# Coarse attention of two heads in three pieces of 96 keys instead of four of 72

## The chip, the cores and the metric

The program runs on one core of a Trainium2 chip. The metric is device time in microseconds (us) of one execution. The engines are TensorE (PE in the rows; PEld is its weight load), VectorE (DVE), ScalarE (ACT), GpSimd (POOL) and SyncE (SP, whose queue issues nearly all DMAs here). They run side by side and wait for one another by semaphores.

## The reference

An attention block feeds two feed-forward layers. q, k and v have 4 batches, 8 heads, 576 tokens and 64 channels, all in float32.

```python
q_d = q.reshape(B, H, Sd, 4, D).mean(axis=3)      # likewise k_d and v_d: Sd = 144 coarse tokens
out_d = softmax(q_d @ k_d.T / sqrt(D)) @ v_d
out_up = np.repeat(out_d, 4, axis=2)
mask = np.abs(pos[:, None] - pos[None, :]) < 4     # local part: a band of seven keys
out_local = softmax(where(mask, q @ k.T / sqrt(D), -1e9)) @ v
x = (out_up + out_local)                           # to (2304, 512)
h = x @ w_in;  x = (h * sigmoid(h)) @ w_out                # first layer, 512 -> 2048 -> 512
h = x @ w2_in; out = (h * sigmoid(1.702 * h)) @ w2_out     # second layer
```

The weights of both layers are given as float64 and are converted on the chip.

## The kernel before, in words

The two layers are float16 products in two parts each (a high and a low half; three products stand for one). They are the lines L709, L840 and L868 (first layer) and L902 and L981 (second layer). The attention is computed in float32. It is cut into 32 units: a unit is one pair of heads (of four, `NHP`) in one half of a batch's queries (eight halves, `NM`), so a unit has 288 queries, of which come 72 coarse queries (`PD` = 72), against 144 coarse keys per head.

A unit runs through these steps, each a small function. `scores` (L1247 coarse, L1254 local) fills a PSUM tile with both kinds of scores. `dmax`, `dexp` and `dnorm` make the coarse probabilities `pd`, a tile of 72 queries by two heads by 144 keys. `dtr` (L1313) transposes it on TensorE in four pieces of 72 keys, two for each head, into one PSUM bank; `dcp` (L1317) copies these to SBUF as `pdT`. `av` (L1330) multiplies each piece by the pooled values `vd` (72 keys by 64 channels): head 0 writes partitions 0 to 63 of the result, head 1 partitions 64 to 127, and the two pieces of a head add up in PSUM. Behind it `av` issues the 24 local products (L1336) on tiles of 32 rows and 64 columns. TensorE carries out each float32 product as two passes, so four coarse products are eight matmuls in the trace; a transpose is one.

The pooled values of a pair of heads are made once per batch. For batch 0 `vsum` (L1198) sums the value windows `vw`, which the local part has loaded anyway, by matmuls with a constant of zeros and ones, `T["vsum"]`, made by a GpSimd memset (L1046) and VectorE reductions (L1052) at the start; `vcp` (L1202) copies the result out of PSUM. For the batches 1 to 3 `lv` (L1091) loads v with four tokens in a row into the tile `vraw`, of which there is one buffer, and `sv` (L1180, L1181) adds the four tokens on GpSimd. The next `lv` waits until `sv` has read the tile.

The order of all steps on all engines is fixed by a string of places (`PLACES`) that lists the steps; the costs noted with each step do not change that order. Each engine works through its own instructions in that order. On SyncE the loads `lv` stand between the loads of k (L1076), q (L1076), value windows (L1125), weights (L523, L604) and the stores of converted weights (L632).

Of the kernel before, what the change touches and what calls it, by code (L numbers as in the profile page):

```python
# [8 lines left out]
F32 = mybir.dt.float32  # L9
# [14 lines left out]
BAND = 4  # L24
# [75 lines left out]
class Plan:  # L100
# [7 lines left out]
    def add(self, name, eng, dur, fn, r=(), w=(), alloc=(), lock=False, mb=0.0, after=(), nd=1):  # L108
        s = Step()
        s.name, s.eng, s.dur, s.fn, s.lock, s.mb = name, eng, dur, fn, lock, mb  # L110
        s.deps, s.succ, s.alloc, s.n, s.nd = {}, [], list(alloc), len(self.steps), nd
        for a in after:
            s.deps[a] = False
        for k in r:
            for p in self.last.get(k, ()):
                s.deps[p] = True
            self.readers.setdefault(k, []).append(s)
        for k in w:
            for p in self.last.get(k, ()):
                s.deps[p] = True  # L120
            for p in self.readers.get(k, ()):
                if p is not s:
                    s.deps[p] = True
            self.last[k] = [s]
            self.readers[k] = []
        for tag, key, *_ in alloc:
            self.tags[key] = tag
        s.keys = set(r) | set(w)
        for k in s.keys:
            self.users.setdefault(k, []).append(s)  # L130
        self.steps.append(s)
        return s
# [87 lines left out]
def kernel(ctx: ExitStack, tc: tile.TileContext, q, k, v, w1_in, w1_out, w2_in, w2_out, out):  # L220

    nc = tc.nc
    B, H, S, D = q.shape
    NT, DM = out.shape
    DFF = w1_in.shape[1] // 2
    P = 128
    NHP = H // 2
# [4 lines left out]
    T2 = 256  # L232
    D2 = DM // 2
    PD = HALF // BAND
    QB = 24
    TT = 96
    NBL = HALF // TT
# [9 lines left out]
    add = plan.add  # L247
# [8 lines left out]
    pools = {}  # L256
    T = {}
# [6 lines left out]
    DVE, ACT, POOL = nc.vector, nc.scalar, nc.gpsimd  # L264
# [758 lines left out]
    def attention_init():  # L1023
        ac = pools["ac"]
        T["ident"] = const.tile([P, P], F32, name="ident")
        make_identity(nc, T["ident"])
        T["cap"] = ac.tile([P, 2 * NBL, 32], F32, name="cap")
        T["big"] = x2[:, 0, 0:P].rearrange("p (i k) -> p i k", i=4)
        POOL.memset(T["big"], 3.0e38)
        for sign in (1, -1):  # L1030
            POOL.affine_select(out=T["big"], in_=T["big"], pattern=[[32 * sign, 4], [sign, 32]], compare_op=ALU.is_ge,
                               fill=8.0 * NEG, base=BAND - 1 - sign * BAND, channel_multiplier=-sign)
        T["kTs"] = [ac.tile([P, S + 2 * BAND], F32, name=f"kT{i}") for i in range(NHP)]
        for t in T["kTs"]:
            POOL.memset(t[:, 0:BAND], 0.0)
            POOL.memset(t[:, BAND + S:], 0.0)
        T["qTs"] = [ac.tile([P, HALF + PD], F32, name=f"qT{i}") for i in range(2)]
        for t in T["qTs"]:
            POOL.memset(t[:, HALF:], 0.0)
        T["smr"] = [ac.tile([P, 8, 2], F32, name=f"smr{i}") for i in range(2)]  # L1040
        T["smi"] = [ac.tile([P, 8], F32, name=f"smi{i}") for i in range(2)]
        for t in T["smr"]:
            POOL.memset(t[:, :, 0], 1.0)
            POOL.memset(t[:, :, 1], 1e-9)
        T["vsum"] = ac.tile([P, 3, PD], F32, name="vsum")
        POOL.memset(T["vsum"], 0.0)  # L1046
        T["four"] = ac.tile([P, TT + 2 * QB], F32, name="four")

    def init_cap():
        cap = T["cap"]  # L1050
        for e in range(3):
            DVE.tensor_reduce(out=T["vsum"][:, e, QB * e:QB * (e + 1)].rearrange("p (i t) -> p i t", i=4),  # L1052
                              in_=T["ident"].rearrange("p (i j) -> p i j", i=4)[:, :, BAND:BAND + QB].rearrange("p i (t r) -> p i t r", r=BAND),
                              axis=AX.X, op=ALU.add)
        DVE.tensor_copy(out=T["four"][:, QB:QB + TT], in_=T["ident"][:, :TT])
        DVE.tensor_reduce(out=T["four"][:, :QB], in_=T["ident"][:, :TT].rearrange("p (t r) -> p t r", r=BAND), axis=AX.X, op=ALU.add)
        DVE.tensor_scalar(out=T["four"][:, QB + TT:], in0=T["four"][:, :QB], scalar1=SCD, scalar2=None, op0=ALU.mult)
        for i in range(4):
            r = slice(32 * i, 32 * i + 32)
            DVE.tensor_copy(out=cap[r], in_=T["big"][r, i, :].unsqueeze(1).to_broadcast([32, 2 * NBL, 32]))  # L1060
        DVE.memset(cap[0:32, 0, 0:BAND], 8.0 * NEG)
        DVE.memset(cap[96:128, 2 * NBL - 1, 32 - BAND:], 8.0 * NEG)
# [16 lines left out]
                nc.sync.dma_start(out=t[:TT].rearrange("p (c h d) -> p c h d", h=2, d=D)[:, :, hh], in_=src[hh].rearrange("(c p) d -> p c d", p=TT))  # L1079

    def load_kv(b, hp):
        h = slice(2 * hp, 2 * hp + 2)
        nm = f"{b}.{hp}"

        def lk():
            T["kraw" + nm] = pools["ld"].tile([P, S + 2 * TT], F32, tag="kraw", name="kraw")
            load_tokens(T["kraw" + nm], [k[b, 2 * hp + hh] for hh in range(2)], S, blocked(2 * b))

        def lv():
            T["vraw" + nm] = pools["ld"].tile([PD, 4, BAND * D], F32, tag="vraw", name="vraw", bufs=1)  # L1090
            nc.sync.dma_start(out=T["vraw" + nm], in_=v[b, h].rearrange("h (c p r) d -> p (h c) (r d)", p=PD, r=BAND))  # L1091

        n0 = len(plan.steps)
        add("lk" + nm, "SP", 0.44, lk, w=["kraw" + nm], alloc=[("kraw", "kraw" + nm)], mb=1.0 if blocked(2 * b) else 0.69, nd=4 if blocked(2 * b) else 2)
        if b:
            add("lv" + nm, "SP", 0.36, lv, w=["vraw" + nm], alloc=[("vraw", "vraw" + nm)], mb=0.33)
        if b:
            for s in plan.steps[n0:]:
                plan.soft.append((w1_loaded, s))
# [51 lines left out]
    def keys_of(b, hp):  # L1151
        nm = f"{b}.{hp}"
        kps, kT, kd, vd = "kps" + nm, "kT" + nm, "kd" + nm, "vd" + nm
# [21 lines left out]
                              in_=src.rearrange("p c (t r) -> p c t r", r=BAND), axis=AX.X, op=ALU.add)  # L1175

        def sv():
            T[vd] = pools["at"].tile([PD, 4, D], F32, tag="vd", name="vd", bufs=NHP)
            vr = T["vraw" + nm].rearrange("p j (r d) -> p j r d", r=BAND)
            POOL.tensor_tensor(out=vr[:, :, 0:2, :], in0=vr[:, :, 0:2, :], in1=vr[:, :, 2:4, :], op=ALU.add)  # L1180
            POOL.tensor_tensor(out=T[vd], in0=vr[:, :, 0, :], in1=vr[:, :, 1, :], op=ALU.add)  # L1181
# [8 lines left out]
        vps = "vps" + nm  # L1190

        def vsum():
            T[vps] = bank1("vps")
            o = T[vps][:PD, :4 * D].rearrange("p (h c d) -> p c h d", h=2, c=2)
            vw = T["vw" + nm].rearrange("p (h c e) d -> p c e h d", h=2, c=2)
            for c in range(2):
                for e in range(3):
                    nc.tensor.matmul(o[:, c], T["vsum"][:, e], vw[:, c, e], start=e == 0, stop=e == 2)  # L1198

        def vcp():  # L1200
            T[vd] = pools["at"].tile([PD, 4, D], F32, tag="vd", name="vd", bufs=NHP)
            ACT.copy(out=T[vd].rearrange("p j d -> p (j d)"), in_=T[vps][:PD, :4 * D])  # L1202

        if b:
            add("KV" + nm, "POOL", 2.1, sv, r=["vraw" + nm], w=[vd], alloc=[("vd", vd)])
# [4 lines left out]
    def unit(u):  # L1210
# [96 lines left out]

        def dtr():
            T[tps] = bank1("tps")
            for hh in range(2):  # L1310
                for kc in range(2):
                    j = 2 * hh + kc
                    nc.tensor.transpose(T[tps][:PD, j * PD:(j + 1) * PD], T[pd][:, hh, kc * PD:(kc + 1) * PD], T["ident"][:PD, :PD])  # L1313

        def dcp():
            T[pdT] = pools["at"].tile([PD, 4, PD], F32, tag="pdT", name="pdT", bufs=1)
            ACT.copy(out=T[pdT].rearrange("p j t -> p (j t)"), in_=T[tps][:PD, :4 * PD])  # L1317

        def ltr():
            T[PT] = pools["at"].tile([P, 2 * NBL, 32], F32, tag="PT", name="PT")  # L1320
# [2 lines left out]
        def av():  # L1323

            T[ul] = [bank1("ul0"), bank1("ul1"), bank2("ul2")]
            ups = T[ul][0][:, HALF:HALF + PD]
            lo = [T[ul][0], T[ul][1], T[ul][2][:, 0, :], T[ul][2][:, 1, :]]
            for hh in range(2):
                for kc in range(2):
                    nc.tensor.matmul(ups[D * hh:D * hh + D, :], T[vd][:, 2 * hh + kc, :], T[pdT][:, 2 * hh + kc, :],  # L1330
                                     start=(kc == 0), stop=(kc == 1))
            for bl in range(NBL):
                for hh in range(2):
                    for i in range(4):
                        r = slice(32 * i, 32 * i + 32)
                        nc.tensor.matmul(lo[i][D * hh:D * hh + D, bl * QB:(bl + 1) * QB], T[vw][r, hh * 2 * NBL + half * NBL + bl, :],  # L1336
                                         T[PT][r, hh * NBL + bl, 0:QB], start=True, stop=True, tile_position=(32 * i, D * hh))
# [222 lines left out]
```

## Time and profile before

| | us |
|---|---|
| median of 3 runs | 882.34 |
| lowest and highest | 881.52, 885.59 |
| profiled execution | 882.64 |
| its span, first to last instruction | 880.9 |

| engine | busy us | share of the span | instructions |
|---|---|---|---|
| PE | 856.5 | 97% | 10204 |
| PEld | 714.5 | 81% | 10204 |
| DVE | 607.4 | 69% | 1306 |
| ACT | 466.9 | 53% | 833 |
| POOL | 159.9 | 18% | 193 |

Busy time of PE counts each matmul from its start to its modelled end, and matmuls overlap, so the start-to-start distance in the timeline tells more than the durations. A row of the timeline merges like instructions of one engine that follow one another: start, time from the first start to the last end, and how many.

### The profile page before, as it was taken

The page shows a single profiled execution, that of the slowest core. Times are in us where ns is not written, and L with a number is a line of the kernel's source. Part 1 is how long each engine was busy: PE and PEld are TensorE (multiplying, and loading weights), DVE is VectorE, ACT ScalarE, POOL GpSimd, SP SyncE. Part 2 cuts the span into 40 slices and gives each one's busy share as a digit, 9 for nine tenths or more (in the row PEclk, how much of TensorE's full clock was granted, in tenths as well). Part 3 has the DMA queues.
Part 4 walks back from the last instruction along what each step waited for, and adds up shares of the span by engine and source line. Part 5 has one row for each costly group of instructions (what it writes and reads, how often), then busy time and mean ns, then how long its engine had stood idle before and what let it go on. Part 6 is the DMA issues. An engine that isn't in the chain of part 4 may idle for free.

```text
span 880.9 us, 23832 instructions
## 1 busy us (share of the span) xinstructions
PE 856.5 (97%) x10204; PEld 714.5 (81%) x10204; DVE 607.4 (69%) x1306; ACT 466.9 (53%) x833; POOL 159.9 (18%) x193
## 2 busy tenths in 40 slices
PE   7779899999999999999999999999999999999998
PEld 6667677777777777777787788888888888888887
DVE  4899998868877666577565889375574738365572
ACT  6989965536556357475553755243342525243341
POOL 1244523031423222112210013000000400002000
PEclk9879999999999999999999999999999999999999
DMA  9986735374455534524226200000000000000000
GB/s 241 262 290 120 203 67 112 61 154 86 111 120 129 144 103 128 147 74 150 69 85 257 97 1 1 25 1 13 2 37 1 25 25 2 25 2 25 1 26 25
DMA packets 114990, 75.86 MB, mean 86 GB/s; under 512 B 94788, under 2 KB 100292, under 8 KB 113860
## 3 DMA queue, kind: packets, MB, share of 16 engines
q1 hardware_dynamic: 114884, 74.34, 31.9%
q8 instruction: 80, 1.31, 0.7%
q14 instruction: 26, 0.21, 0.1%
HBM read 61.21 MB, written 13.11 MB: 84 GB/s over the span
## 4 chain that ended last, share of the span: by engine, by line
PE 83%; DVE 9%; DMA 4%; ACT 2%; issue 1%; POOL 0%; SPq 0%; DVEq 0%; ACTq 0%
PE hps L902 21%; PE ops L840 19%; PE hps L709 18%; PE oy L981 10%; PE oz L981 5%; PE ox L981 2%; PE ul L1336 2%; PE sl L1254 1%; DMA kraw<-in_k_dram 1%; PE sl L1247 1%; PE ul L1330 1%; DVE wout L382 1%; DMA st<-in_moe_w_in_dram 1%; DVE tg L724 1%; DVE g L930 1%
## 5 line engine op out<-in xcount | busy, mean ns | idle before, releaser
L709 PE MATMUL hps<-xhl,win 128*128 128x288 f16 x1536 | 198.4, 287 | 2.5 <-DVE tg L724 1.6
L902 PE MATMUL hps<-xhl,win 128*128 128x256 f16 x1728 | 190.4, 273 | 0.1
L902 PEld LDWEIGHTS <-win 128*128 128x128 f16 x1728 | 169.1, 98 | 20.0 <-issue 0.4
L709 PEld LDWEIGHTS <-win 128*128 128x128 f16 x1536 | 148.4, 98 | 40.5 <-issue 3.1
L840 PE MATMUL ops<-g,wout 128*128 128x288 f16 x1344 | 170.7, 286 | 0.0
L981 PEld LDWEIGHTS <-g 128*128 128x128 f16 x1512 | 147.7, 98 | 20.0 <-issue 2.2
L840 PEld LDWEIGHTS <-wout 128*128 128x128 f16 x1344 | 129.5, 98 | 33.0 <-issue 0.6
L914 ACT ACTIVATE tg<-hps,blk 128x512 f32<-128x512 f32 x72 | 49.5, 687 | 127.6 <-PE hps L902 118.4
L917 DVE SCALAR_TENSOR_TENSOR tg<-tg,hps 128x512 f32<-128x512 f32 x72 | 49.1, 682 | 61.0 <-ACT tg L914 61.0
L930 DVE SCALAR_TENSOR_TENSOR g<-tg,g 128x896 f16<-128x896 f32 x72 | 78.6, 1103 | 0.5
L981 PE MATMUL oy<-wout,g 128*128 128x256 f16 x648 | 75.1, 272 | 0.3 <-ACT o L959 0.3
L927 ACT ACTIVATE g<-tg 128x896 f16<-128x896 f32 x72 | 67.6, 944 | 14.5 <-DVE tg L923 9.1
L921 POOL TENSOR_TENSOR tg<-tg 128x128 f32<-128x128 f32 x17 | 11.2, 660 | 348.8 <-DVE tg L917 348.8
L721 ACT ACTIVATE tg<-hps,blk 128x576 f32<-128x576 f32 x64 | 47.0, 734 | 30.7 <-PE hps L709 22.6
L350 POOL TENSOR_TENSOR cs<-cs,cz 128x512 int32<-128x512 int32 x32 | 42.4, 1327 | 108.8 <-DVE cs L333 61.5
L724 DVE SCALAR_TENSOR_TENSOR tg<-tg,hps 128x576 f32<-128x576 f32 x64 | 47.8, 746 | 19.3 <-ACT tg L721 19.1
L731 ACT ACTIVATE g<-tg,gs 128x576 f16<-128x576 f32 x56 | 42.6, 769 | 23.4 <-DVE tg L724 22.4
L734 DVE SCALAR_TENSOR_TENSOR g<-tg,gs,g 128x576 f16<-128x576 f32 x56 | 47.7, 862 | 5.7 <-ACT g L731 5.1
L959 ACT ACTIVATE o<-oy,blk 128x256 f32<-128x256 f32 x27 | 12.7, 470 | 65.5 <-PE oy L981 65.5
L965 DVE SCALAR_TENSOR_TENSOR o<-oy,blk,o 128x256 f32<-128x256 f32 x9 | 4.4, 484 | 60.7 <-issue 39.2
L350 POOL TENSOR_TENSOR x<-x,z 128x512 int32<-128x512 int32 x21 | 31.4, 1513 | 52.6 <-PE sps L562 26.3
L325 ACT ACTIVATE st<-st 128x512 f32<-128x512 f32 (+1 forms) x48 | 39.4, 826 | 1.3 <-DMA st<-in_moe_w_out_dram 1.1
(172 smaller groups left out, 1166.8 us busy)
## 6 DMA issues: line engine op xcount, KB each, us to landing
st<-in_moe_w_in_dram SPq DMA_DIRECT2D x8, 1024.0 KB
st<-in_moe_w_out_dram SPq DMA_DIRECT2D x8, 1024.0 KB
st<-in_moe_w_in_dram SPq DMA_DIRECT2D x16, 512.0 KB
st<-in_moe_w_out_dram SPq DMA_DIRECT2D x16, 512.0 KB
vw<-in_v_dram SPq DMA_DIRECT2D x62, 96.0 KB
out_dram<-o SPq DMA_DIRECT2D x18, 256.0 KB
wdin<-cs SPq DMA_DIRECT2D x16, 256.0 KB
r<-wdin SPq DMA_DIRECT2D x4, 1024.0 KB
```

What stands on the lines that cost most here:

```text
L350: eng.tensor_tensor(out=s, in0=s, in1=zget()[:, o], op=ALU.add)
L709: nc.tensor.matmul(o, T[w][:, kc, a, fc * P:(fc + 1) * P], T[xk][:, kc, b, :T_], start=(n == 0), stop=(n == 3 * KC - 1))
L721: ACT.activation(out=T[tg], in_=T[ps][:, :, :T_], func=AF.Tanh, scale=T["a" + sk][:, c:c + 1])
L724: DVE.scalar_tensor_tensor(out=T[tg], in0=T[tg], scalar=1.0, in1=T[ps][:, :, :T_], op0=ALU.add, op1=ALU.mult)
L734: DVE.scalar_tensor_tensor(out=T[g][:, 1], in0=T[tg], scalar=gs, in1=T[g][:, 0], op0=ALU.mult, op1=ALU.subtract)
L840: nc.tensor.matmul(o, w[:, j, a, dc * P:(dc + 1) * P], g[:, b, j % 2, :], start=(n == 0), stop=(n == 3 * NF - 1))
L902: nc.tensor.matmul(o, T[w][:, kc, a, fc * P:(fc + 1) * P], T[xk][:, kc, b, :], start=(n == 0), stop=(n == 3 * KC - 1))
L914: ACT.activation(out=four(), in_=T[ps][:, 0, :], func=AF.Tanh, scale=T["a" + bk][:, c:c + 1])
L917: DVE.scalar_tensor_tensor(out=four(), in0=four(), scalar=1.0, in1=T[ps][:, 0, :], op0=ALU.add, op1=ALU.mult)
L927: ACT.activation(out=T[g][:, 0], in_=T[tg], func=AF.Copy, scale=GS2)
L930: DVE.scalar_tensor_tensor(out=T[g][:, 1], in0=T[tg], scalar=GS2, in1=T[g][:, 0], op0=ALU.mult, op1=ALU.subtract)
L981: nc.tensor.matmul(T[bank[acc]], g[:, a, slot, :], w, start=first and p == p0 and i == 0, stop=prod in (2, 3, 4) and p == NF // 2 - 1 and ...
```

## The change

The two heads' 288 coarse keys are cut into three pieces of 96 (`KR` = 96) instead of four of 72. Piece 0 holds 96 keys of head 0, piece 2 holds 96 keys of head 1, and piece 1 holds the last 48 keys of head 0 and the first 48 of head 1. `dtr` makes three transposes of 96 key columns. `vd` has four blocks of 64 channels on 96 partitions: head 0 for piece 0, head 0 for piece 1 (zero on the partitions of head 1's keys), head 1 for piece 1 (zero on those of head 0), head 1 for piece 2. In `av` pieces 0 and 2 are products of 64 columns each, and piece 1 is one product of 128 columns that adds into both heads' partitions. `vsum` sums the windows into this arrangement with twelve products of 64 columns in place of six of 128; its constant has four blocks of 96 columns. `lv` is four DMAs instead of one, into a `vraw` that is kept for the whole attention and is cleared once at the start, since the two middle blocks keep zeros on half of their partitions.

```diff
--- before.py
+++ after.py
@@ -232,6 +232,7 @@
     T2 = 256
     D2 = DM // 2
     PD = HALF // BAND
+    KR = 4 * PD // 3
     QB = 24
     TT = 96
     NBL = HALF // TT
@@ -1042,13 +1043,15 @@
         for t in T["smr"]:
             POOL.memset(t[:, :, 0], 1.0)
             POOL.memset(t[:, :, 1], 1e-9)
-        T["vsum"] = ac.tile([P, 3, PD], F32, name="vsum")
+        T["vsum"] = ac.tile([P, 4, KR], F32, name="vsum")
         POOL.memset(T["vsum"], 0.0)
+        T["vraw"] = ac.tile([KR, 4, BAND * D], F32, name="vraw")
+        POOL.memset(T["vraw"][:, 1:3], 0.0)
         T["four"] = ac.tile([P, TT + 2 * QB], F32, name="four")
 
     def init_cap():
         cap = T["cap"]
-        for e in range(3):
+        for e in range(4):
             DVE.tensor_reduce(out=T["vsum"][:, e, QB * e:QB * (e + 1)].rearrange("p (i t) -> p i t", i=4),
                               in_=T["ident"].rearrange("p (i j) -> p i j", i=4)[:, :, BAND:BAND + QB].rearrange("p i (t r) -> p i t r", r=BAND),
                               axis=AX.X, op=ALU.add)
@@ -1079,7 +1082,6 @@
                 nc.sync.dma_start(out=t[:TT].rearrange("p (c h d) -> p c h d", h=2, d=D)[:, :, hh], in_=src[hh].rearrange("(c p) d -> p c d", p=TT))
 
     def load_kv(b, hp):
-        h = slice(2 * hp, 2 * hp + 2)
         nm = f"{b}.{hp}"
 
         def lk():
@@ -1087,13 +1089,18 @@
             load_tokens(T["kraw" + nm], [k[b, 2 * hp + hh] for hh in range(2)], S, blocked(2 * b))
 
         def lv():
-            T["vraw" + nm] = pools["ld"].tile([PD, 4, BAND * D], F32, tag="vraw", name="vraw", bufs=1)
-            nc.sync.dma_start(out=T["vraw" + nm], in_=v[b, h].rearrange("h (c p r) d -> p (h c) (r d)", p=PD, r=BAND))
+            t = T["vraw" + nm] = T["vraw"]
+            src = [v[b, 2 * hp + hh].rearrange("(t r) d -> t (r d)", r=BAND) for hh in range(2)]
+            n, half = 2 * PD, KR // 2
+            nc.sync.dma_start(out=t[:, 0], in_=src[0][0:KR])
+            nc.sync.dma_start(out=t[0:half, 1], in_=src[0][KR:n])
+            nc.sync.dma_start(out=t[half:KR, 2], in_=src[1][0:half])
+            nc.sync.dma_start(out=t[:, 3], in_=src[1][half:n])
 
         n0 = len(plan.steps)
         add("lk" + nm, "SP", 0.44, lk, w=["kraw" + nm], alloc=[("kraw", "kraw" + nm)], mb=1.0 if blocked(2 * b) else 0.69, nd=4 if blocked(2 * b) else 2)
         if b:
-            add("lv" + nm, "SP", 0.36, lv, w=["vraw" + nm], alloc=[("vraw", "vraw" + nm)], mb=0.33)
+            add("lv" + nm, "SP", 1.4, lv, w=["vraw" + nm], alloc=[("vraw", "vraw" + nm)], mb=0.33, nd=4)
         if b:
             for s in plan.steps[n0:]:
                 plan.soft.append((w1_loaded, s))
@@ -1175,7 +1182,7 @@
                               in_=src.rearrange("p c (t r) -> p c t r", r=BAND), axis=AX.X, op=ALU.add)
 
         def sv():
-            T[vd] = pools["at"].tile([PD, 4, D], F32, tag="vd", name="vd", bufs=NHP)
+            T[vd] = pools["at"].tile([KR, 4, D], F32, tag="vd", name="vd", bufs=NHP)
             vr = T["vraw" + nm].rearrange("p j (r d) -> p j r d", r=BAND)
             POOL.tensor_tensor(out=vr[:, :, 0:2, :], in0=vr[:, :, 0:2, :], in1=vr[:, :, 2:4, :], op=ALU.add)
             POOL.tensor_tensor(out=T[vd], in0=vr[:, :, 0, :], in1=vr[:, :, 1, :], op=ALU.add)
@@ -1191,15 +1198,14 @@
 
         def vsum():
             T[vps] = bank1("vps")
-            o = T[vps][:PD, :4 * D].rearrange("p (h c d) -> p c h d", h=2, c=2)
-            vw = T["vw" + nm].rearrange("p (h c e) d -> p c e h d", h=2, c=2)
-            for c in range(2):
-                for e in range(3):
-                    nc.tensor.matmul(o[:, c], T["vsum"][:, e], vw[:, c, e], start=e == 0, stop=e == 2)
+            vw = T["vw" + nm].rearrange("p (h w) d -> p h w d", h=2)
+            for j, (hh, w0, first, n) in enumerate(((0, 0, 0, 4), (0, 4, 0, 2), (1, 0, 2, 2), (1, 2, 0, 4))):
+                for e in range(n):
+                    nc.tensor.matmul(T[vps][:KR, j * D:(j + 1) * D], T["vsum"][:, first + e], vw[:, hh, w0 + e], start=e == 0, stop=e == n - 1)
 
         def vcp():
-            T[vd] = pools["at"].tile([PD, 4, D], F32, tag="vd", name="vd", bufs=NHP)
-            ACT.copy(out=T[vd].rearrange("p j d -> p (j d)"), in_=T[vps][:PD, :4 * D])
+            T[vd] = pools["at"].tile([KR, 4, D], F32, tag="vd", name="vd", bufs=NHP)
+            ACT.copy(out=T[vd].rearrange("p j d -> p (j d)"), in_=T[vps][:KR, :4 * D])
 
         if b:
             add("KV" + nm, "POOL", 2.1, sv, r=["vraw" + nm], w=[vd], alloc=[("vd", vd)])
@@ -1307,14 +1313,13 @@
 
         def dtr():
             T[tps] = bank1("tps")
-            for hh in range(2):
-                for kc in range(2):
-                    j = 2 * hh + kc
-                    nc.tensor.transpose(T[tps][:PD, j * PD:(j + 1) * PD], T[pd][:, hh, kc * PD:(kc + 1) * PD], T["ident"][:PD, :PD])
+            p = T[pd].rearrange("p h k -> p (h k)")
+            for j in range(3):
+                nc.tensor.transpose(T[tps][:KR, j * PD:(j + 1) * PD], p[:, j * KR:(j + 1) * KR], T["ident"][:PD, :PD])
 
         def dcp():
-            T[pdT] = pools["at"].tile([PD, 4, PD], F32, tag="pdT", name="pdT", bufs=1)
-            ACT.copy(out=T[pdT].rearrange("p j t -> p (j t)"), in_=T[tps][:PD, :4 * PD])
+            T[pdT] = pools["at"].tile([KR, 3, PD], F32, tag="pdT", name="pdT", bufs=1)
+            ACT.copy(out=T[pdT].rearrange("p j t -> p (j t)"), in_=T[tps][:KR, :3 * PD])
 
         def ltr():
             T[PT] = pools["at"].tile([P, 2 * NBL, 32], F32, tag="PT", name="PT")
@@ -1325,10 +1330,9 @@
             T[ul] = [bank1("ul0"), bank1("ul1"), bank2("ul2")]
             ups = T[ul][0][:, HALF:HALF + PD]
             lo = [T[ul][0], T[ul][1], T[ul][2][:, 0, :], T[ul][2][:, 1, :]]
-            for hh in range(2):
-                for kc in range(2):
-                    nc.tensor.matmul(ups[D * hh:D * hh + D, :], T[vd][:, 2 * hh + kc, :], T[pdT][:, 2 * hh + kc, :],
-                                     start=(kc == 0), stop=(kc == 1))
+            w = T[vd].rearrange("p j d -> p (j d)")
+            for j, (rows, cols) in ((0, (slice(0, D), slice(0, D))), (2, (slice(D, P), slice(3 * D, 4 * D))), (1, (slice(0, P), slice(D, 3 * D)))):
+                nc.tensor.matmul(ups[rows, :], w[:, cols], T[pdT][:, j, :], start=j != 1, stop=j == 1)
             for bl in range(NBL):
                 for hh in range(2):
                     for i in range(4):
```

## Rows read from the trace of the kernel before

**Rows 1.** Busy time by stage: window, length, each engine's busy us, PEclk, DMA share.

```profile
core 0: us, PE busy (x) PEld busy (x) DVE busy (x) ACT busy (x) POOL busy (x), PEclk, DMA share, GB/s
20.00:65.00 45.00, 34.86 (x578) 29.71 (x571) 40.42 (x98) 40.68 (x68) 15.56 (x10) 0.74 0.99 268
65.00:105.00 40.00, 36.29 (x680) 27.99 (x678) 39.55 (x94) 36.81 (x67) 18.27 (x19) 1.00 0.74 166
105.00:145.00 40.00, 39.61 (x561) 31.27 (x560) 37.93 (x93) 25.64 (x53) 15.55 (x17) 1.00 0.53 112
145.00:438.00 293.00, 292.56 (x4271) 229.69 (x4272) 209.88 (x500) 165.33 (x373) 67.39 (x67) 1.00 0.45 111
```

**Rows 2.** Waits of PE from 105 to 438 us: total, times, longest.

```profile
PE sl L1247 <- DVE xf L1351: 0.4, 1, 0.4
PE rm L781 <- DVE dg L776: 0.4, 1, 0.4
```

**Rows 3.** Timeline of PE around one unit's `av`, from 125 and from 131.89 us.

```profile
125.90 6.05 PE L868 MATMUL ops<-g,wout 128*128 128x288 f16 x48
...
131.67 0.29 PE L868 MATMUL ops<-g,wout 128*128 128x288 f16 x1
...
131.88 0.33 PEld L1330 LDWEIGHTS ul<-pdT,vd 72*64 72x64 f32 x8 [0.24 <-issue]
131.88 0.48 PE L1330 MATMUL ul<-pdT,vd 72*64 72x72 f32 x8
...
132.29 0.13 PEld L1336 LDWEIGHTS ul<-PT,vw 32*64 32x64 f32 x1
```

**Rows 4.** Lines L1330 and L1313 from 105 to 438 us: ns minimum/median/maximum.

```profile
L1330 PE MATMUL ul<-pdT,vd x192: 226/226/278, 117.7 to 435.7; 72*64 72x72 f32 x192
...
L1313 PE MATMUL tps<-ident,pd x96: 223/225/258, 111.0 to 430.9; 72*72 72x72 f32 x96
```

**Rows 5.** Timeline of PE around one unit's transposes.

```profile
158.88 0.41 PE L1313 MATMUL tps<-ident,pd 72*72 72x72 f32 x4
159.14 1.15 PE L709 MATMUL hps<-xhl,win 128*128 128x288 f16 x8
```

**Rows 6.** Timeline of PE: `kps` and `vps` groups at the high clock.

```profile
23.12 1.50 PE L1159 MATMUL kps<-four,kraw 96*128 96x120 f32 x12
24.45 1.48 PE L1198 MATMUL vps<-vw,vsum 128*72 128x128 f32 x12
```

**Rows 7.** Timeline of the start: the constant for `vsum`.

```profile
3.03 0.28 POOL L1046 MEMSET vsum<- 128x216 f32 x1
...
3.34 0.57 DVE L1052 TENSOR_REDUCE vsum<-ident 128x24 f32<-128x96 f32 x3 [3.34 <-POOL vsum L1046]
```

**Rows 8.** Chain that ended last, up to 62 us: the `vps` groups on it.

```profile
14.04 2.47 PE vps L1198 x12
...
47.56 2.56 PE vps L1198 x12
```

**Rows 9.** Chain that ended last, from 122 us: transfers of v.

```profile
122.59 4.68 DMA vraw<-in_v_dram
...
131.24 4.23 DMA vw<-in_v_dram
```

**Rows 10.** Timeline of SP, POOL and PE, 129 to 147 us.

```profile
129.43 0.31 SPq L1091 DMA_DIRECT2D vraw<-in_v_dram  x1
129.83 1.88 SPq L1125 DMA_DIRECT2D vw<-in_v_dram  x4
...
136.34 0.31 SPq L1091 DMA_DIRECT2D vraw<-in_v_dram  x1
...
143.53 1.27 POOL L1180 TENSOR_TENSOR vraw<-vraw 72x512 f32<-72x512 f32 x1
144.87 0.72 POOL L1181 TENSOR_TENSOR vd<-vraw 72x256 f32<-72x256 f32 x1
146.88 0.34 PE L1330 MATMUL ul<-pdT,vd 72*64 72x72 f32 x3
```

## Prediction

> **What bounds the kernel now.** First the busy time by stage. From 105 to 438 us TensorE is busy 39.61 of 40 and 292.56 of 293 us while every other engine has air [rows 1]; its waits there, read next, come to 0.8 us in two places [rows 2]. So in that stretch each nanosecond of TensorE's stream is a nanosecond of the whole, and nothing else is. From 65 to 105 us VectorE is the full one (39.55 of 40), TensorE is not (36.29). From 20 to 65 us the DMA engines are full (share 0.99), VectorE and ScalarE are at nine tenths, and TensorE runs at a mean granted clock of 0.74, so partly at 1.2 GHz [rows 1]. Behind 438 us no step of the change runs.
>
> The attention has 32 units (a unit is one pair of heads in one half of a batch). Eight of 256 coarse products are one unit's, so 192 of them, 24 units, lie behind 105 us [rows 4]. The change is decided there, unit by unit.
>
> **The coarse products (`av`), the largest term.** A unit issues four f32 products, each as two passes: eight matmuls of 64 columns. The rows of one unit [rows 3]: the last f16 matmul before them starts at 131.67 and streams for some 0.123 us (48 in 6.05 us), to 131.79. The first weight load of `av` and its matmul start at 131.88: TensorE stands for 0.09 us although nothing is waited for. The eight matmuls, 0.226 us each, stretch over 0.48, so their starts lie within 0.25 us. One 72-column f32 matmul takes 0.062 us of streaming (four transposes in 0.41 us of 0.225 each, [rows 5]), so eight in a row would need 0.43: they run two at a time, the one head in array columns 0 to 63, the other in 64 to 127, four rounds. The first weight load shows in full: 278 against 226 ns, 0.052 us for 64 columns [rows 4]. Sum: 0.09 + 0.052 + 4 x 0.062 + 0.014 (offset of the pair) = 0.405, then 0.09 more before the next load at 132.29, where the local products change to tiles of 32 rows.
>
> After the change pieces 0 and 2 still run side by side: 2 rounds, 0.138. Piece 1 is 128 columns wide and fills the array. So a third change of shape enters each unit. I price it by the two that the rows show: 0.09 of standing, then a weight load with nothing to hide behind. Its size: at the high clock twelve `kps` matmuls of 120 columns with 128 weight columns take 1.50 us of 0.275 each, 0.111 apiece, while `vps` with more moving columns (128) and 72 weight columns takes 0.110 [rows 6]; so the 128-column f32 load, some 0.107 to 0.111, sets `kps`'s pace (for 64 columns 0.052 fits that). Two passes need two loads; the first is in sight, the second starts when the first matmul does and ends 0.045 after it. Piece 1: 0.09 + 0.107 + 0.062 + 0.045 + 0.062 = 0.366. New sum 0.09 + 0.052 + 0.138 + 0.366 = 0.646 before the local products' own 0.09: **+0.24 us a unit**. Bounds: 0, if every load hides and nothing pauses (not below: piece 1's two passes can't run side by side, so 2 + 2 rounds remain four); and +0.24, which has the full pause and both loads. I take the upper end, since both neighbouring changes of shape stand for the same 0.09.
>
> The Trainium skill's "TensorEngine Tiling (Array Packing)", section "Key Properties", says that changing the tiling mode drains TensorE. No row here shows a change from half-width to full-width products of 128 rows; by the rule it pays as above. The page "TensorE: Matmul & The Clock Gate", section "Step-by-step: what each phase is for", says the engine pulls weight loads ahead of running matmuls; by it alone piece 1's first load would hide, which is the second rival. Against it: the first load of each `av` has no f16 matmul over it in [rows 3].
>
> **The transposes (`dtr`).** Four of 72 columns become three with 96 weight columns. Four take 159.14 - 158.88 = 0.26 us between f16 matmuls, without a pause at either side [rows 5], 0.062 to 0.065 each. The longest one, with its load in sight, is 258 against 225 ns: 0.033 for 72 columns [rows 4], so 96 columns load in about 0.044, under the 0.062 of streaming. One fewer: **-0.062 us a unit**. Were a load twice that (as in `av`), the gain would be 0.02; bounds -0.02 to -0.065.
>
> Net, 24 units x (0.243 - 0.062) = **+4.3 us** (bounds -1.6 and +5.4). The four units between 65 and 105 us have TensorE idle beside them: +0.3 of 0.7.
>
> **ScalarE and GpSimd.** `dcp` copies 216 instead of 288 columns, some 0.06 us of ScalarE a unit; ScalarE is 165 of 293 busy [rows 1], so nothing. `sv` works on 96 partitions with the same elements in each: nothing.
>
> **The start.** `init_cap` has a fourth reduction (0.57 us for three, so 0.19) and waits for a memset that grows from 216 to 384 elements (0.28, so about 0.1 more) [rows 7]: +0.3, ahead of the first `kps`. The memset of `vraw` is behind it on GpSimd, which then idles: hidden. `vsum` has 24 matmuls with 64 moving and 96 weight columns instead of 12 with 128 and 72. If the load sets the pace (0.08 each at the high clock, 0.16 at the low), a group goes from 1.3 to 2.0 us, and at the low clock from 2.56 to 3.84. The lower bound is 0 (twice as many, half as long). The first and the last of the four groups stand on the chain of waits with 2.47 and 2.56 us [rows 8]: up to +1.3 each; the two others sit between waits. With 0.18 for each of the first four units the chain carries 0.3 + 2.6 + 0.7 = 3.6 us. In front of 65 us, though, transfers fill the DMA engines: weight tiles that are asked for later arrive with less beside them. I take half: **+1.8** (0.3 to 3.6).
>
> **The loads of v (`lv`).** One issue of 0.31 us becomes four; four issues of `vw` take 1.88 [rows 10], so +1.4 on SP per load, and the `vw` loads behind it move too. `vraw` has one buffer: the next `lv` waits for `sv`. Of batch 1 three loads follow each other at once: transfer 4.68, `sv` 1.27 + 0.72, next `lv`, next `vw` 4.23 [rows 9, 10]. The last of them ends at 145.59 and its `av` starts at 146.88: 1.3 us of slack against 3 x 1.4 = 4.2 of delay, of which GpSimd's own queue hides some (the last load was issued at 136.34 and `sv` begins at 143.53, seven us later, where 4.7 was the transfer) and TensorE's delay some. `vw` comes 2.8 later, and the maximum over it feeds the `rm` matmul, which already waits 0.4 [rows 2]. I take **+0.8** (0 to 3). For batches 2 and 3 TensorE waits for nothing [rows 2] and the loads come early: 0.
>
> **Sum** against the profiled execution (882.64 us, span 880.9, 0.3 above the 882.34 median): 4.3 + 0.3 + 1.8 + 0.8 = +7.2, so 889.8, or **889.5 us** on the median's scale.
>
> **Rivals.**
> 1. Other side: TensorE streams through the change of width. Then `av` keeps four rounds, -0.062 x 24 = -1.5, the start and `lv` hide behind their covers but for 0.3 and a little: 881 us. For it: pairs of 64-column products already share the 128-row array with no pause between rounds [rows 3]. Against: the pause on entering exactly that pairing from full width. It decides if piece 1 starts within 0.06 us of the last round's end.
> 2. The array drains, but piece 1's first load hides in the drain or under the last round: +0.08 to +0.137, less 0.062, is +0.4 to +1.8 us over 24 units, with the other terms 885.6 to 887.
> 3. The `lv` chain decides: the 4.2 us of delay reach TensorE at 146.9 with 3 us: 892.
> 4. The vsum groups pass on in full: 891.3.
>
> **How the numbers follow.** Forecast 0.57, within 886 to 893 by the bounds of start and `lv`; rival 2 0.17; rival 1 0.13; rivals 3 and 4 together 0.13. What a measurement of this kernel tells from no change is about 0.5%, 4.4 us: slower means above 886.8, faster below 877.9. Faster needs rival 1 and a gain in `av` too: 0.06. Within: the rest of rival 1 (0.07), most of rival 2 (0.13), a low forecast (0.06): 0.26. Slower 0.68. Range 882 to 894: it leaves out most of rival 1 below and a late `lv` above.
>
> **What would show it.** In the rows after: in each unit behind 105 us a pause of 0.09 us between the fourth 64-column matmul of `av` and the first of 128 columns, and 0.6 us instead of 0.41 from the first `av` matmul to the local products; three transposes in 0.19 instead of four in 0.26; `vsum` groups of 24 in 2 to 4 us; a wait of TensorE near 145 us. Wrong I am if `av` stays within 0.45 us, or if TensorE waits more than 3 us behind 105 us.

## The result and the profile after

| | median us | runs, lowest to highest | profiled span |
|---|---|---|---|
| before | 882.41 | 6, 881.23 to 885.59 | 880.9 |
| changed | 890.57 | 6, 888.54 to 891.73 | 889.4 |

The ratio is 1.0086, 95% interval [1.0073, 1.0100]: 8.2 us slower, where 889.5 was forecast (+7.2). The total came out as forecast; its parts did not all. Lines of the changed kernel are a few higher: the transposes are L1318, `av` is L1335, the local products L1340, `vsum` L1204.

Busy time by stage of the changed kernel (columns as in [rows 1]):

```profile
core 0: us, PE busy (x) PEld busy (x) DVE busy (x) ACT busy (x) POOL busy (x), PEclk, DMA share, GB/s
...
20.00:65.00 45.00, 42.34 (x566) 37.99 (x567) 36.54 (x90) 38.23 (x68) 11.26 (x8) 0.85 0.85 231
...
105.00:145.00 40.00, 39.32 (x550) 30.98 (x548) 39.38 (x89) 27.38 (x54) 13.22 (x14) 1.00 0.42 105
145.00:438.00 293.00, 292.85 (x4182) 229.26 (x4180) 207.52 (x499) 160.71 (x366) 70.16 (x71) 1.00 0.45 114
```

From 20 to 65 us TensorE went from 34.86 [rows 1] to 42.34 us busy of 45, while VectorE and ScalarE got less done: the start now waits for TensorE above all, as the chain below shows. Its waits from 105 us to the end of the attention answer to [rows 2]:

```profile
PE spo L578 <- DVE sum_out L581: 0.6, 1, 0.6
```

Both waits of before are gone, and there is none near 145 us for v (the 0.6 is a matmul that waited 0.6 in the kernel before too, just ahead of 105 us).

One unit's `av` in the changed kernel, answering to [rows 3]; the second fence is of a window that ends ahead of piece 1, the third of one that begins when the four matmuls ahead of piece 1 have ended:

```profile
174.05 0.41 PE L710 MATMUL hps<-xhl,win 128*128 128x288 f16 x2
174.39 0.72 PE L1335 MATMUL ul<-pdT,vd 96*64 96x72 f32 x6
175.03 0.24 PE L1340 MATMUL ul<-PT,vw 32*64 32x24 f32 x3
```

```profile
174.39 0.35 PE L1335 MATMUL ul<-pdT,vd 96*64 96x72 f32 x4
```

```profile
174.66 0.33 PE L1335 MATMUL ul<-pdT,vd 96*128 96x72 f32 x1
```

From the first `av` matmul to the first local one it is 175.03 - 174.39 = 0.64 us, where the kernel before took 132.29 - 131.88 = 0.41. Four half-width matmuls end within 0.35, so the last of them starts at 174.51 (0.35 less its 0.226) and, at 0.062 us of streaming, is through by 174.57. The first of full width starts at 174.66: the pause of 0.09 us that was forecast. Line L1335 over all 24 units (ns minimum/median/maximum, forms):

```profile
L1335 PE MATMUL ul<-pdT,vd x144: 226/276/330, 122.4 to 443.9; 96*64 96x72 f32 x96, 96*128 96x72 f32 x48
```

The longest is 330 against 226: a 128-column weight load shows in full, 0.104 us; 278 was the longest before [rows 4]. The transposes, answering to [rows 5]:

```profile
163.81 0.35 PE L1318 MATMUL tps<-ident,pd 72*96 72x72 f32 x3
164.00 1.27 PE L710 MATMUL hps<-xhl,win 128*128 128x288 f16 x9
```

Three take 0.19 us where four took 0.26. The chain of the changed kernel up to 70 us (start, length, what), answering to [rows 8]:

```profile
14.24 3.80 PE vps L1204 x24
...
25.55 2.56 PE kps L1166 x12
...
28.11 3.79 PE vps L1204 x24
...
37.39 3.84 PE vps L1204 x24
...
51.39 3.80 PE vps L1204 x24
```

All four `vsum` groups stand on the chain, not two, and each takes 3.8 us.

To split the 8.5 us of the span, the fifth unit's local products (the first past the start) and the last unit's are laid against those of before. Timeline of PE, before:

```profile
66.19 0.71 PE L1336 MATMUL ul<-PT,vw 32*64 32x24 f32 x48
...
435.83 0.71 PE L1336 MATMUL ul<-PT,vw 32*64 32x24 f32 x48
```

and changed:

```profile
71.13 0.71 PE L1340 MATMUL ul<-PT,vw 32*64 32x24 f32 x48
...
444.09 0.71 PE L1340 MATMUL ul<-PT,vw 32*64 32x24 f32 x48
```

The start is 4.9 us late, the last unit 8.3: the rest, 3.3 us, came in behind it: 0.18 us from one unit to the next behind 118 us, except where the two waits went. Between the fifth unit and the ninth (the first behind 105 us; its local products start at 118.06 before and at 123.02 now, 5.0 us late) nothing was added.

### The profile page after: what moved, and what is told of

It is laid out like the page before. It is cut to its first block, busy times and chain, and to the rows that moved or that the text cites. A ratio compares the mean times of both kernels' runs of the same rounds, so it can differ in the third digit from the quotient of the medians.

```text
span 889.4 us, 23793 instructions
## 1 busy us (share of the span) xinstructions
PE 873.5 (98%) x10156; PEld 729.8 (82%) x10156; DVE 606.2 (68%) x1307; ACT 465.4 (52%) x833; POOL 157.6 (18%) x194
## 4 chain that ended last, share of the span: by engine, by line
PE 90%; DVE 6%; DMA 1%; ACT 1%; issue 1%; POOL 0%; DVEq 0%; POOLq 0%; ACTq 0%
PE hps L903 21%; PE ops L841 19%; PE hps L710 18%; PE oy L982 10%; PE oz L982 5%; PE ops L869 3%; PE ox L982 2%; PE ul L1335 2%; PE ul L1340 2%; PE vps L1204 2%; PE sl L1260 2%; PE kps L1166 1%; PE sl L1253 1%; DMA st<-in_moe_w_out_dram 1%; DVE g L931 1%
## 5 line engine op out<-in xcount | busy, mean ns | idle before, releaser
L351 POOL TENSOR_TENSOR x<-x,z 128x512 int32<-128x512 int32 x21 | 28.4, 1374 | 58.1 <-PE sps L563 38.4
```

The source lines that it names most:

```text
L351: eng.tensor_tensor(out=s, in0=s, in1=zget()[:, o], op=ALU.add)
```

## The experiments

Each ratio is to the kernel before, measured beside the experiment. The "start" below is the fifth unit's local products against 66.19, in one profile each. Experiments 4 and 5 leave `vsum` as it was before, and yet their starts are 0.50 and 1.05 us late, so a start that differs by 1 us or less is not read as an effect:

```profile
66.69 0.71 PE L1338 MATMUL ul<-PT,vw 32*64 32x24 f32 x48
```

```profile
67.24 0.71 PE L1343 MATMUL ul<-PT,vw 32*64 32x24 f32 x48
```

**1. Piece 1 in two halves.** In the changed kernel:

```diff
-            for j, (rows, cols) in ((0, (slice(0, D), slice(0, D))), (2, (slice(D, P), slice(3 * D, 4 * D))), (1, (slice(0, P), slice(D, 3 * D)))):
-                nc.tensor.matmul(ups[rows, :], w[:, cols], T[pdT][:, j, :], start=j != 1, stop=j == 1)
+            for j, piece, rows in ((0, 0, slice(0, D)), (1, 1, slice(0, D)), (3, 2, slice(D, P)), (2, 1, slice(D, P))):
+                nc.tensor.matmul(ups[rows, :], w[:, j * D:(j + 1) * D], T[pdT][:, piece, :], start=j in (0, 3), stop=j in (1, 2))
```

> The changed kernel, but piece 1 in av is two products of 64 columns, one for each head, so that all four products stay of half width and run side by side. Theory (a third change of shape in each unit costs a pause of 0.09 us and two 128-column weight loads, 0.24 us a unit): av takes 0.41 us again instead of 0.65, 24 units behind 105 us give back 5.8 us and the first eight up to 0.7: 884 to 885 us. What is left over the kernel before (2 us) is the start, +4.7 less 1.5 from the transposes and 0.8 of waits gone. Rival (the loss sits in the start and in the loads of v, not in av): 889 or more. Rival (64-column products with 96 rows don't run side by side): above 890.

885.58 us, ratio 1.0031 [1.0021, 1.0040]: just above the expected 884 to 885, and 5.0 us less than the changed kernel with two more matmuls in each unit. Its `av`:

```profile
172.97 0.48 PE L1335 MATMUL ul<-pdT,vd 96*64 96x72 f32 x8
173.38 0.52 PE L1340 MATMUL ul<-PT,vw 32*64 32x24 f32 x34
```

0.41 us, as before the change, so 96 rows pair as 72 did. Its start is 70.33, 4.1 us late, and its last unit (438.37 against 435.83) only 2.5: what remains of the loss is in the start.

**2. Piece 1 first.** The same instructions as the changed kernel, in another order:

```diff
-            for j, (rows, cols) in ((0, (slice(0, D), slice(0, D))), (2, (slice(D, P), slice(3 * D, 4 * D))), (1, (slice(0, P), slice(D, 3 * D)))):
-                nc.tensor.matmul(ups[rows, :], w[:, cols], T[pdT][:, j, :], start=j != 1, stop=j == 1)
+            for j, (rows, cols) in ((1, (slice(0, P), slice(D, 3 * D))), (0, (slice(0, D), slice(0, D))), (2, (slice(D, P), slice(3 * D, 4 * D)))):
+                nc.tensor.matmul(ups[rows, :], w[:, cols], T[pdT][:, j, :], start=j == 1, stop=j != 1)
```

> The changed kernel with the same three products in av in another order: piece 1 (128 columns) first, right behind the f16 matmuls of the same shape, then pieces 0 and 2. Theory (the change of shape is what costs): one change fewer, the first 128-column load hides under the f16 matmul before it; av is 0.17 + 0.09 + 0.052 + 0.138 = 0.45 us instead of 0.65, 24 x 0.2 = 4.7 us less: 885.5 to 886. Rival (only the 128-column load costs, no pause): 0.107 less a unit, 888. Rival (the number of passes is what counts): 890.6, no change, since the instructions are the same.

885.20 us, ratio 1.0033 [1.0021, 1.0046]. The order alone is worth 5.4 us. Its `av`, whose first matmul now starts while the f16 stream runs:

```profile
172.27 1.02 PE L710 MATMUL hps<-xhl,win 128*128 128x288 f16 x7
173.12 0.62 PE L1335 MATMUL ul<-pdT,vd 96*128 96x72 f32 x6
173.67 0.44 PE L1340 MATMUL ul<-PT,vw 32*64 32x24 f32 x30
```

The last f16 matmul starts 0.286 us, its own length, ahead of the end of its group: at 173.00 here, at 174.17 in the changed kernel. From there to the local products it is 0.67 us here and 0.86 there: 0.19 less, where 0.20 was computed. Over all 24 units no matmul shows a 128-column load any more; the longest is 277 ns, where it was 330:

```profile
L1335 PE MATMUL ul<-pdT,vd x144: 226/250/277, 121.9 to 438.7; 96*64 96x72 f32 x96, 96*128 96x72 f32 x48
```

Its start is 70.92, 4.7 us late, and its last unit (438.90) 3.1: here, too, what remains is in the start. Neither the number of passes nor the width of piece 1 by itself costs the 0.24 us; the change of shape in the middle does, with the first load that it lays bare.

**3. `vsum` with six products.** In the changed kernel (the coarse values of batch 0 are then not the reference's):

```diff
-            for j, (hh, w0, first, n) in enumerate(((0, 0, 0, 4), (0, 4, 0, 2), (1, 0, 2, 2), (1, 2, 0, 4))):
-                for e in range(n):
-                    nc.tensor.matmul(T[vps][:KR, j * D:(j + 1) * D], T["vsum"][:, first + e], vw[:, hh, w0 + e], start=e == 0, stop=e == n - 1)
+            o = T[vps][:KR, :4 * D].rearrange("p (h c d) -> p c h d", h=2, c=2)
+            for c in range(2):
+                for e in range(3):
+                    nc.tensor.matmul(o[:, c], T["vsum"][:, e], vw[:, :, 3 * c + e], start=e == 0, stop=e == 2)
```

> The changed kernel, but vsum issues six products of 128 moving columns for batch 0, as before the change, in place of twelve of 64; the weights still have 96 columns. The coarse values of batch 0 are left out of their right places by this. Theory (the 96-column load sets the pace of the 24 matmuls, 0.16 us each at the low clock, and the groups stand on the chain of the start): a group goes from 3.63 us back to 2.56 at the low clock, the start gives back 1.3 for each of the two groups on the chain, some 2.5 us in all: 888; the steady part behind 105 us keeps its 0.18 us a unit. Rival (the start is late by the clock or by the constants, not by vsum): within 0.5 us of 890.6.

885.83 us, ratio 1.0035 [1.0022, 1.0048]: 4.7 us less, nearly twice what I expected, on the side of the theory; the expectation counted two groups, and the chain of the changed kernel has four. Its groups, and its fifth unit:

```profile
14.21 2.77 PE L1205 MATMUL vps<-vw,vsum 128*96 128x128 f32 x12
25.19 1.48 PE L1205 MATMUL vps<-vw,vsum 128*96 128x128 f32 x12
35.40 2.87 PE L1205 MATMUL vps<-vw,vsum 128*96 128x128 f32 x12
47.63 1.98 PE L1205 MATMUL vps<-vw,vsum 128*96 128x128 f32 x12
```

```profile
65.73 0.71 PE L1341 MATMUL ul<-PT,vw 32*64 32x24 f32 x48
```

The start is 0.5 us early, within its scatter, with the longer `init_cap`, the larger memsets and the new `av` all in place: the 4.9 us come with `vsum` in 24 matmuls.

**4. `lv` as four DMAs, in the kernel before.**

```diff
-            T["vraw" + nm] = pools["ld"].tile([PD, 4, BAND * D], F32, tag="vraw", name="vraw", bufs=1)
-            nc.sync.dma_start(out=T["vraw" + nm], in_=v[b, h].rearrange("h (c p r) d -> p (h c) (r d)", p=PD, r=BAND))
+            t = T["vraw" + nm] = pools["ld"].tile([PD, 4, BAND * D], F32, tag="vraw", name="vraw", bufs=1)
+            src = v[b, h].rearrange("h (c p r) d -> p (h c) (r d)", p=PD, r=BAND)
+            for j in range(4):
+                nc.sync.dma_start(out=t[:, j], in_=src[:, j])
```

> The kernel before with one part of the change alone: lv as four DMAs instead of one (into the same tile of 72 partitions). Theory (SP has room for the three more issues; the loads of v reach av in time): 882.4, within 0.3%. Rival (the three loads of batch 1 follow each other, 1.4 us later each, and TensorE waits for them near 145 us): 884.5 to 885.5, with a wait of 1 to 3 us of TensorE for a product or the rm matmul there.

882.16 us, ratio 0.9991 [0.9982, 1.0000]: not slower. In the changed kernel the first load of batch 1 (the first and the last of its four issues, and `sv`), then the third load (its first issue, `sv` and the `av` that needs it):

```profile
127.31 0.45 SPq L1095 DMA_DIRECT2D vraw<-in_v_dram  x1
...
128.74 0.42 SPq L1098 DMA_DIRECT2D vraw<-in_v_dram  x1
...
130.99 1.27 POOL L1187 TENSOR_TENSOR vraw<-vraw 96x512 f32<-96x512 f32 x1 [4.74 <-DMA vraw<-in_v_dram]
...
140.65 0.32 SPq L1095 DMA_DIRECT2D vraw<-in_v_dram  x1
...
147.69 1.27 POOL L1187 TENSOR_TENSOR vraw<-vraw 96x512 f32<-96x512 f32 x1
149.04 0.72 POOL L1188 TENSOR_TENSOR vd<-vraw 96x256 f32<-96x256 f32 x1
...
151.57 0.72 PE L1335 MATMUL ul<-pdT,vd 96*64 96x72 f32 x6
```

From the first issue to `sv` of the first load it is 3.7 us, with one DMA 4.75 (from 122.59 [rows 9] to `sv` at 127.34): the four queue behind one another on SP, but their transfers overlap with the issuing. Four DMAs are not faster as a rule: of the loads that `sv` waited for, those around 225 us took 4.0 us with one and 5.3 with four (issue at 222.08 and `sv` at 226.09; 227.64 and 232.92). In the third load, the tight one, `sv` did not wait for the transfer at all: from issue to `sv` it is 7.0 us here and was 143.53 - 136.34 = 7.2 [rows 10]. The slack of the tightest unit was 1.3 us [rows 10] and is 151.57 - 149.76 = 1.8.

**5. Batch 0 as before, three pieces behind it, piece 1 in halves.**

```diff
-            for j in range(3):
-                nc.tensor.transpose(T[tps][:KR, j * PD:(j + 1) * PD], p[:, j * KR:(j + 1) * KR], T["ident"][:PD, :PD])
+            n, kr = (3, KR) if b else (4, PD)
+            for j in range(n):
+                nc.tensor.transpose(T[tps][:kr, j * PD:(j + 1) * PD], p[:, j * kr:(j + 1) * kr], T["ident"][:PD, :PD])
```

with the same choice in `dcp`; `vsum`, its constant and `vcp` as before the change; and `av` as in experiment 1, which in batch 0 takes pieces 0 and 1 for head 0, 2 and 3 for head 1.

> Units of batch 0 as before the change (four pieces of 72, vsum of six products), units of the batches 1 to 3 in three pieces with piece 1 as two products of 64 columns. Theory (of the change only the missing transpose is worth something): the start is that of the kernel before, av is as long as before, and each of 24 units gives back 0.062 us: 1.5 us less than before, 881.1 us, ratio 0.998. Rival (another engine sets the pace once TensorE has less to do): 882.5, no change.

881.29 us, ratio 0.9986 [0.9977, 0.9996]: the gain is there and is as small as one transpose a unit. In its trace the lead over the kernel before grows by 0.06 us from one unit to the next behind 150 us, with one exception near 230 us.

**6. Piece 1 in halves, `vsum` in eight products.** `av` is that of experiment 1. Pieces 0 and 2 use the same block of the constant, so one product of 128 columns serves both (`w` is the tile `vw`; the lines of `vsum` that these replace are left out):

```diff
+            o = T[vps][:KR, :4 * D].rearrange("p (j d) -> p j d", j=4)
+            for e in range(4):
+                nc.tensor.matmul(o[:, 0:4:3], T["vsum"][:, e], w[:, e:e + 9:8], start=e == 0, stop=e == 3)
+            for j, w0, first in ((1, 4, 0), (2, 6, 2)):
+                for e in range(2):
+                    nc.tensor.matmul(o[:, j], T["vsum"][:, first + e], w[:, w0 + e], start=e == 0, stop=e == 1)
```

> The changed kernel with piece 1 as two products, and vsum in eight products: four of 128 columns that serve pieces 0 and 2 together, four of 64 for the middle, all with 96 weight columns. Theory (the length of the vsum groups passes on to the start in full): at the low clock a group takes 8 x 0.213 + 8 x 0.16 = 3.0 us, between 2.56 and 3.84; the start is late by a third of what 24 matmuls cost, some 1.5 us of 4.7, and behind it the transposes give 1.5 back: 882 to 883.5 us. Rival (the start is late as soon as a group is longer at all, by the clock's phase): 885, as with 24 matmuls.

881.25 us, ratio 0.9983 [0.9974, 0.9992], a little below the expected 882 to 883.5. Its groups and its fifth unit:

```profile
14.03 1.92 PE L1204 MATMUL vps<-vw,vsum 128*96 128x128 f32 x8
15.74 1.30 PE L1207 MATMUL vps<-vw,vsum 128*96 128x64 f32 x8
24.92 1.04 PE L1204 MATMUL vps<-vw,vsum 128*96 128x128 f32 x8
25.79 0.81 PE L1207 MATMUL vps<-vw,vsum 128*96 128x64 f32 x8
...
67.11 0.71 PE L1343 MATMUL ul<-PT,vw 32*64 32x24 f32 x48
```

The first group is 3.0 us as computed, the second at the high clock 1.7. The start is 0.9 us late, which is within its scatter, so this run does not show by itself what a slightly longer group costs; it rules out the rival's 885. This and experiment 5 beat both kernels; between the two the runs can't choose.

## Why the prediction was right, and which terms were mis-sized

**`av`: right in mechanism and size.** +0.24 us a unit was worked out; 0.64 against 0.41 us is measured. The pause shows in the fences above. From the end of the half-width streaming at 174.57 it is 0.36 us to 174.94, which is 0.09 ahead of the local products, and 0.09 + 0.104 + 0.062 + 0.045 + 0.062 = 0.36 is just that. Experiments 1 and 2 take the change of shape away, once with more matmuls and once with the same ones, and 5.0 and 5.4 us go: 24 x 0.24 = 5.8 and 24 x 0.2 = 4.7 were expected. The rule of the Trainium skill's "TensorEngine Tiling (Array Packing)", "Key Properties", that a change of tiling mode drains TensorE, held for the one change that no row of before showed, with 0.09 us. The other rule of the Trainium skill that was weighed, that weight loads are pulled ahead ("TensorE: Matmul & The Clock Gate", "Step-by-step: what each phase is for"), holds in experiment 2, where the load follows a matmul of its own shape, and not across a change of shape in the changed kernel: 330 against 226 ns.

**Transposes: right.** -0.062 us a unit; 0.19 against 0.26 us. Experiment 5 has them without the longer `av` and the longer `vsum`: 1.2 us at the medians, 1.5 expected.

**The steady part came to +3.3 instead of +4.6 us** (4.3, and 0.3 for the units ahead of 105 us). The units up to the first behind 105 us added nothing, and the two waits of 0.4 us [rows 2] are gone: 23 x 0.18 = 4.1, less 0.8. I had used the waits as evidence that nothing waits, and did not take them off the sum.

**The start was mis-sized: +1.8 forecast, +4.9 measured**, near rival 4, whose 3.6 it exceeds, and outside the range of 0.3 to 3.6 that the step had. `init_cap` was the small part: the first `kps` matmul starts at 4.54 us instead of 4.38, 0.16 late, where 0.3 was forecast. Two things failed in that step. First, "the two others sit between waits": they took 3.8 us at half pace, outlasted what had covered them and joined the chain. Second, the half that was taken off because "transfers fill the DMA engines": the share stayed at 1.02 from 20 to 50 us and was 0.35 from 50 to 60 (last fence), where it had been 0.64, and the start is later than the whole chain of rival 4. That the weights' loads wait for tiles which ScalarE and VectorE free, and these for TensorE, is how I read the chain; no run tests it. The delay goes with the length of the groups. Timeline of PE before (the second group is in [rows 6]), and in experiment 1:

```profile
13.84 2.67 PE L1198 MATMUL vps<-vw,vsum 128*72 128x128 f32 x12
...
34.88 2.43 PE L1198 MATMUL vps<-vw,vsum 128*72 128x128 f32 x12
...
47.36 2.77 PE L1198 MATMUL vps<-vw,vsum 128*72 128x128 f32 x12
```

```profile
14.28 3.99 PE L1204 MATMUL vps<-vw,vsum 128*96 128x64 f32 x24
26.36 2.18 PE L1204 MATMUL vps<-vw,vsum 128*96 128x64 f32 x24
35.90 4.10 PE L1204 MATMUL vps<-vw,vsum 128*96 128x64 f32 x24
50.09 3.99 PE L1204 MATMUL vps<-vw,vsum 128*96 128x64 f32 x24
```

Together 9.35 us before and 14.26 in experiment 1: 4.9 longer, and the start is 4.1 late. In the changed kernel, with 24 in some 4.0 us four times, they are 6.7 longer and the start is 4.9 late; in experiment 3 they are 0.25 shorter (9.10) and it is 0.5 early. Length is not all that differs, and the runs do not separate the two: where `vsum` has 24 matmuls, others also run at half pace for longer. The third `kps` group takes 2.77 us in experiment 1 (from 41.16) and 1.50 before (from 37.80), and in the changed kernel three of the first four `av` take 1.07 us to the local products, where the prediction had 0.18 more for a whole unit.

**`lv`: +0.8 forecast, 0 measured**, and rival 3 with it: I added three issues for each of three loads, but the first reached `sv` 1 us sooner after its first issue, and in the third `sv` starts seven us behind the issue either way. The prediction named GpSimd's own queue and counted it for too little.

The misses, +3.1 in the start, -1.3 in the steady part and -0.8 in `lv`, partly cancel; that the total is within 1.1 us of the forecast is owed to that as much as to `av`. What stays open is why TensorE ran the second group at half pace in the changed kernel: in experiment 1, with the same `vsum`, the second ran at full pace (24 in 2.18 us).

## What to carry to other kernels

Count the changes of shape between neighbouring matmuls, not the matmuls: a product that is wider, fuller and one fewer can cost more than the two it replaces, and next to matmuls of its own shape it cost 0.05 us a unit here (0.67 us in experiment 2, 0.62 before) instead of 0.24. For small f32 products take the pace from the weight load as well as from the moving columns, and where a few of them stand in a start at the low clock, count their whole length as late unless a wait of that length is shown to follow. A high busy share of the DMA engines was no cover here.

## What the runs showed of the hardware

- A change between products of 128 and of 64 columns on 128-row tiles cost TensorE 0.09 us of standing in either direction (131.79 to 131.88 us before [rows 3], 174.57 to 174.66 us in the changed kernel), and the first weight load behind it shows in full (278 and 330 ns against 226).
- An f32 weight load shows as 0.052 us for 64 columns and 0.104 for 128 at 2.4 GHz, which is two clocks a column; with 96 columns this fits `vsum`'s spacing, (3.99 - 0.36) / 23 = 0.158 us at half pace (row below) and (2.18 - 0.25) / 23 = 0.084 at full pace in experiment 1 (0.36 and 0.25 us are the lengths of each group's last matmul). The load ahead of a transpose shows about half that: 0.033 for 72 columns [rows 4], and 0.044 for 96 in the changed kernel (268 against 224 ns).
- The granted clock of a stretch can be shown as full where the matmuls run at half pace: in the changed kernel it stands at 1.00 from 20 to 50 us, while its `kps` groups there take 2.77 us and the same twelve matmuls took 1.50 before [rows 6]. The spacing of like matmuls is the safer reading.

Timeline of PE of the changed kernel, and its windows from 20 to 50 and from 50 to 60 us (columns as in [rows 1]):

```profile
25.34 2.77 PE L1166 MATMUL kps<-four,kraw 96*128 96x120 f32 x12
27.90 3.99 PE L1204 MATMUL vps<-vw,vsum 128*96 128x64 f32 x24
```

```profile
20.00:50.00 30.00, 29.19 (x404) 26.97 (x404) 24.19 (x56) 24.79 (x44) 5.64 (x5) 1.00 1.02 267
50.00:60.00 10.00, 8.15 (x89) 7.51 (x90) 7.38 (x26) 8.52 (x17) 2.91 (x3) 0.54 0.35 123
```
